# A gated recurrence and a convolutional gate on one core: fixed issue orders, tile-sized loads and word transposes

## Chip, cores and metric

One of the eight cores of a Trainium2 chip runs the kernel. The metric is the device time of one launch in microseconds. The kernel before was run 13 times: median 320.02 us, from 318.58 to 324.23. Engines are named as in the profile: PE multiplies matrices (PEld loads its weights), DVE is VectorE, ACT is ScalarE, POOL is GpSimd, and SP only issues DMAs here.

## Reference, cut to what matters

Input x and two gates are (4, 6336, 256) float32. A linear recurrence over time is followed by a gated unit whose gate is a causal convolution of five taps:

```python
log_a = 8.0 * sigmoid(r_gate) * log(clip(sigmoid(a_param), 1e-6, 1 - 1e-6))
a_t = exp(log_a)
x_gated = sqrt(maximum(1 - a_t * a_t, 1e-6)) * sigmoid(i_gate) * x
for t in range(S):
    h = a_t[:, t] * h + x_gated[:, t]
    y[:, t] = h
gate_pre = sum(conv_w[k] * shifted(y, 4 - k) for k in range(5))   # zeros before t = 0
out = (sigmoid(gate_pre) * (y @ w_val)) @ w_out
```

## The kernel before

The four sequences are laid end to end: 25344 rows of 256 values. They are cut into 51 tiles, 48 of 512 rows and 3 of 256, and the tiles into 28 chunks: 23 of two tiles (1024 rows) and five of one. Rows lie in partitions where data is loaded and stored; channels lie in partitions, in two halves h of 128, where the recurrence and the convolution run. So data is transposed by PE on the way in.

One tile or chunk goes through these operations, each a function `op_...` in the code:

- **load** (chunk, SP, L249 and L250): r_gate and i_gate into `ri`, two buffers of a chunk (NIN). **loadx** (chunk, SP, L257): x into `xt`, three buffers (NX). The pattern of r_gate, `(w p j) d -> p w j d`, gives each partition four neighbouring rows of a tile, 4 KB in one piece; that of i_gate and x, `(k p) d -> p k d`, gives it single rows of 1 KB.
- **tanh** (tile, ACT, L351): both gates at once, into bf16 rings.
- **u2** (tile): (tanh(i) + 1) * x into `uring`, bf16. A string of letters, U2, says for each tile whether DVE does it in one instruction (L360) or POOL in two (L363, L364).
- **srT** (half a chunk, PE, L332): eight bf16 transposes of 128x128 of tanh(r) into a PSUM bank; **exp** (ACT, L376) makes a of it, and puts time in order as it reads; **e** (POOL, L384) squares a.
- **sq** (batches of one to three chunks, UNITS; ACT, L388): the square root, in place in `ering`, as bf16 (`nring`). The root and tanh/exp need different function tables, so a table load (ACT_TABLE_LOAD) stands on either side of a batch.
- **nT** (tile, PE, L397): eight bf16 transposes back to rows; **xg** (DVE, L404) multiplies them into `uring`; **xT** (half a chunk, PE, L332 again): eight transposes to channels; **scan** (DVE, L425): the recurrence, from `aring` and the PSUM bank into `yring`.
- **conv** (tile, PE, L451): the five taps as products with diagonal matrices; **tg** (ACT, L459): tanh of the gate; **val** (PE, L467): y times w_val; **gv** (DVE, L477): (tg + 1) * val.
- **out** (piece of 256 rows, PE, L489): times w_out; **osb** (evicts PSUM; a string OSB says on DVE, L500, or on ACT, L502); **store** (tile, SP, L507).

w_out is halved once at the start (DVE, L313), since sigmoid(z) = (tanh(z/2) + 1) / 2.

Four PSUM banks are shared by srT, nT, xT and out. What sets the order is a planner run when the program is built: `make_jobs` lists all jobs with a duration from a table COST and what they depend on, and `make_plan` always takes the job that can start first, ties going by a table PRIO. The jobs are written out by planned start, so each engine, and SP's queue, has one fixed order and waits in it for its semaphores. The first six load jobs of the plan are issued ahead of the setup work.

Of the kernel before, what the change touches and what calls it, by code (L numbers as in the profile page):

```python
# [18 lines left out]
UNITS = [1, 2, 2, 3, 3, 3, 3, 3, 2, 2, 1, 3]  # L19
# [4 lines left out]
NIN = 2  # L24
NX = 3
# [7 lines left out]
OSB = ("ADDDDDDDDDDDDADDDDDDDDDDDDADDDDDDDDADDDDDDDDDADDDDAADDADDDDDDADDADDDDAADDAAADADADADADADADA"  # L33
       "DAAAAAAAA")

U2 = "PDPDDDDDDPDPDPDPDDPDPPPPPPPPPPPPPPPDPPPPPPPDPPPPPPP"

COST = dict(load=(0.05, 2.8), loadx=(0.02, 1.5), tanh=(0.2, 1.7), u2P=(0.25, 3.15), u2D=(0.2, 1.55), srT=(0.05, 0.45), exp=(0.35, 0.86), e=(0.1, 1.8),
            sq=(0.3, 1.71), nT=(0.05, 0.47), xg=(0.1, 0.58), xT=(0.05, 0.45), scan=(0.21, 2.14), conv=(0.2, 1.1), tg=(0.19, 0.83),
            val=(0.02, 0.93), gv=(0.15, 1.07), out=(0.02, 0.47), osbD=(0.68, 0), osbA=(0.59, 0),  # L40
            store=(0.05, 1.3))
PRIO = dict(load=5.92, loadx=5.97, store=2.53, tanh=6, exp=2.8, sq=0.42, tg=-0.32, srT=-1.6, nT=0.31, xT=3.79,
            conv=5.3, val=4.34, out=2.99, e=5.93, u2=6, xg=4.55, scan=0.36, gv=-0.61, osb=-0.99)
# [66 lines left out]
def make_jobs(sh):  # L110
# [3 lines left out]
    jobs = {op: [] for op in PRIO}  # L114
# [8 lines left out]
    for g, (_, n) in enumerate(sh.tiles):  # L123
        f = n / WIN
        c = sh.chunk_of[g]
        job("tanh", "ACT", f, [("load", c), ("u2", g - NTI)]
            + ([("srT", 2 * sh.chunk_of[g - NTR] + 1)] if g >= NTR else []))
        job("u2", "DVE" if U2[g] == "D" else "POOL", f, [("tanh", g), ("loadx", c)] + ([("xT", 2 * sh.chunk_of[g - NU] + 1)] if g >= NU else []), "u2" + U2[g])
        job("nT", "PE", f, [("sq", unit_of[c]), ("xg", g - PB["nT"])], None, 1)
        job("xg", "DVE", f, [("nT", g), ("u2", g)])  # L130
        job("conv", "PE", f, [("scan", 2 * c + 1), ("tg", g - 1)])
        job("tg", "ACT", f, [("conv", g), ("gv", g - 2)])
        job("val", "PE", f, [("scan", 2 * c + 1), ("gv", g - 1), ("conv", g)])
        job("gv", "DVE", f, [("tg", g), ("val", g)] + ([("out", qlast[g - 2])] if g >= 2 else []))
        job("store", "DMA", f, [("osb", q) for q, (w, _) in enumerate(sh.pieces) if w == g])
    for c, (_, n, g0, g1) in enumerate(sh.chunks):
        f = n / CHUNK
        job("load", "DMA", 2 * f, [("tanh", sh.chunks[c - NIN][3] - 1 if c >= NIN else -1)])
        job("loadx", "DMA", 2 * f, [("u2", sh.chunks[c - NX][3] - 1 if c >= NX else -1)])
# [20 lines left out]
def make_plan(sh):  # L160

    jobs = make_jobs(sh)
    reads = dict(exp="srT", xg="nT", scan="xT", osb="out")
    nxt = dict.fromkeys(jobs, 0)
    done, free, order, mode = {}, dict(DMA=START, ACT=ACT_START), [], "E"
    bank_free, banks = [0.0] * BANKS, {}
    while True:
        best = None  # L170
        for op, todo in jobs.items():
            i = nxt[op]
            if i == len(todo):
                continue
            eng, dur, deps, need = todo[i]
            t = free.get(eng, 0.0)
            if need:
                b = min(bank_free)
                if b == math.inf:
                    continue  # L180
                if b:
                    t = max(t, b + SEM)
            for d in deps:
                e = done.get(d)
                if e is None:
                    break
                if e + SEM > t:
                    t = e + SEM
            else:
                if best is None or (t, PRIO[op]) < best[:2]:  # L190
                    best = (t, PRIO[op], op, i, eng, dur, need)
        if best is None:
            break
        t, _, op, i, eng, dur, need = best
        if eng == "ACT" and op != "osb":
            if (op == "sq") != (mode == "S"):
                dur += TABLE
            mode = "S" if op == "sq" else "E"
        free[eng] = t + dur
        done[op, i] = t + dur + (DMA_LAT if eng == "DMA" else 0.0)  # L200
        if need:
            banks[op, i] = bank_free.index(min(bank_free))
            bank_free[banks[op, i]] = math.inf
        if op in reads:
            bank_free[banks[reads[op], i]] = t + dur
        order.append((t, op, i, eng, dur))
        nxt[op] += 1
    assert all(nxt[op] == len(todo) for op, todo in jobs.items()), nxt
    order.sort(key=lambda o: o[0])
    return order, banks  # L210
# [3 lines left out]
def kernel(  # L214
# [29 lines left out]
    def load(c):  # L244
        t0, nt, g0, g1 = chunks[c]
        nw, nj = g1 - g0, nt // (g1 - g0) // P
        ri = inp.tile([P, 2, 2, SUB, D], FP32, name="ri", tag="ri", bufs=NIN)

        nc.sync.dma_start(ri[:, 0, 0:nw, 0:nj, :], rf[t0:t0 + nt, :].rearrange("(w p j) d -> p w j d", w=nw, j=nj))  # L249
        nc.sync.dma_start(ri[:, 1, 0:nw, 0:nj, :].rearrange("p w j d -> p (w j) d"),  # L250
                          if_[t0:t0 + nt, :].rearrange("(k p) d -> p k d", p=P))
        live["ri", c] = ri

    def loadx(c):
        t0, nt, g0, g1 = chunks[c]
        xt = inp.tile([P, 2 * SUB, D], FP32, name="xt", tag="xt", bufs=NX)
        nc.sync.dma_start(xt[:, 0:nt // P, :], xf[t0:t0 + nt, :].rearrange("(k p) d -> p k d", p=P))  # L257
        live["xt", c] = xt

    with tc.manual_schedule():  # L260
# [5 lines left out]
        before = [(op, g) for _, op, g, eng, _ in plan if eng == "DMA"][:6]  # L266
# [46 lines left out]
        nc.vector.tensor_scalar(out=wo[:], in0=wo[:], scalar1=0.5, scalar2=None, op0=ALU.mult)  # L313
# [4 lines left out]
        def bank(b, dtype):  # L318
            return psum.tile([P, WIN * 4 // mybir.dt.size(dtype)], dtype, name=f"bank{b}", tag=f"bank{b}", bufs=1)
# [5 lines left out]
        uring = rings.tile([P, NU, SUB, D], BF16, name="uring")  # L325
        yring = rings.tile([P, H, NY * WIN], BF16, name="yring")

        def transposes(dst, srcs, h):
            col = 0
            for src, nj in srcs:  # L330
                for j in range(nj):
                    nc.tensor.transpose(out=dst[:, col:col + P], in_=src[:, j, h * P:(h + 1) * P],  # L332
                                        identity=ident_b[:])
                    col += P
# [9 lines left out]
        def op_tanh(g, eng):  # L344
            nj = tiles[g][1] // P
            c = chunk_of[g]
            ri, w = live["ri", c], g - chunks[c][2]
            if g == chunks[c][3] - 1:
                del live["ri", c]
            r, i = g % NTR, NTR + g % NTI  # L350
            nc.scalar.activation(out=tring[:, r:i + 1:i - r, 0:nj, :], in_=ri[:, :, w, 0:nj, :], func=ACT.Tanh, scale=0.5)  # L351

        def op_u2(g, eng):
            nj = tiles[g][1] // P
            c = chunk_of[g]
            w = g - chunks[c][2]
            xt, ti = live["xt", c][:, w * nj:(w + 1) * nj, :], tring[:, NTR + g % NTI, 0:nj, :]
            u = uring[:, g % NU, 0:nj, :]
            if eng == "DVE":
                nc.vector.scalar_tensor_tensor(out=u, in0=ti, scalar=1.0, in1=xt, op0=ALU.add, op1=ALU.mult)  # L360
                return
            t1 = work.tile([P, SUB, D], FP32, name="t1", tag="t1", bufs=1)[:, 0:nj, :]
            nc.gpsimd.tensor_scalar(out=t1, in0=ti, scalar1=1.0, scalar2=1.0, op0=ALU.mult, op1=ALU.add)  # L363
            nc.gpsimd.tensor_tensor(out=u, in0=t1, in1=xt, op=ALU.mult)  # L364

        def op_srT(k, eng):
            c, h = k // 2, k % 2
            srT = bank(banks["srT", k], BF16)
            transposes(srT, [(tring[:, g % NTR], tiles[g][1] // P) for g in range(*chunks[c][2:])], h)
# [21 lines left out]
        def op_nT(g, eng):  # L391
            c = chunk_of[g]
            n0, nt = shape.npos[c] + tiles[g][0] - chunks[c][0], tiles[g][1]
            nT = bank(banks["nT", g], BF16)[:].rearrange("p (j d) -> p j d", d=D)
            for h in range(H):
                for j in range(nt // P):
                    nc.tensor.transpose(out=nT[:, j, h * P:(h + 1) * P],  # L397
                                        in_=nring[:, h, n0 + j * P:n0 + (j + 1) * P], identity=ident_b[:])
            live["nT", g] = nT

        def op_xg(g, eng):
            nj = tiles[g][1] // P
            u = uring[:, g % NU, 0:nj, :]
            nc.vector.tensor_tensor(out=u, in0=live.pop(("nT", g))[:, 0:nj, :], in1=u, op=ALU.mult)  # L404

        def op_xT(k, eng):
            c, h = k // 2, k % 2
            xT = bank(banks["xT", k], BF16)
            transposes(xT, [(uring[:, g % NU], tiles[g][1] // P) for g in range(*chunks[c][2:])], h)
# [8 lines left out]
        def op_scan(k, eng):  # L418
# [4 lines left out]
            xT = live.pop(("xT", k))  # L423
# [59 lines left out]
        def op_out(q, eng):  # L483
            g, i = pieces[q]
            gv = live["gv", g]
            ops = bank(banks["out", q], FP32)
# [6 lines left out]
        def op_osb(q, eng):  # L493
# [5 lines left out]
            if eng == "DVE":  # L499
                nc.vector.tensor_copy(out=dst, in_=ops[:])  # L500
            else:
                nc.scalar.copy(out=dst, in_=ops[:])  # L502
# [42 lines left out]
```

## Time and profile before

One execution was profiled; it took 320.02 us, which happens to be the median, and its span from the first to the last instruction is 318.2 us.

| what | value |
|---|---|
| profiled execution | 320.02 us |
| its span | 318.2 us |
| busy ACT, DVE, PE, POOL | 290.7, 270.4, 245.8, 225.0 us |
| DMA: bytes, mean rate | 104.55 MB, 329 GB/s |
| tanh L351, 128x2048 | 48 of 1914 ns |
| e L384, 128x1024 | 46 of 1974 ns |
| u2 on POOL, L363 and L364, 128x1024 | 33 of 1161 + 2419 ns |
| u2 on DVE, L360, 128x1024 | 15 of 1646 ns |
| eviction on DVE L500, on ACT L502 | 69 of 677 ns, 30 of 584 ns |
| table loads | 26 of 1283 ns |
| scan L425, 128x1024 | 40 of 2337 ns |

How to read it: a line of the profile names line, engine, operation, output and inputs, then the count, the busy time and the mean duration. The slices cut the span in 40 equal parts of 8 us; a digit is the busy share in tenths. Lines of waits give who waited for whom, the total in us, how often, and the longest. The chain follows the work that ended last back from the end. DMA packets are the pieces that one DMA engine moves in one go; their records tell their size and how long each took.

### The profile page before, as it was taken

How to read it: one execution, taken by the hardware profiler on the slowest of the kernel's cores; microseconds unless marked ns; L12 is line 12 of the kernel's file. 1: busy time of each engine (PE TensorE's matmuls, PEld its weight loads, DVE VectorE, ACT ScalarE, POOL GpSimd, SP SyncE). 2: the span in 40 equal slices, each digit the busy share in tenths (PEclk: the TensorE clock that was granted, in tenths of full speed). 3: DMA queues.
4: the chain of work that ended last, by engine and by line, in shares of the span. 5: the costliest groups of instructions: out<-in, count | busy, mean ns of one | idle time of the engine just before them, and what ended most of it. 6: DMA issues, size and time to landing. Idle time of an engine off the chain costs nothing.

```text
span 318.2 us, 7194 instructions
## 1 busy us (share of the span) xinstructions
PE 245.8 (77%) x2954; PEld 163.3 (51%) x2987; DVE 270.4 (85%) x269; ACT 290.7 (91%) x231; POOL 225.0 (71%) x140
## 2 busy tenths in 40 slices
PE   1262976686588768897989788968977997989994
PEld 1141744453465446464746475637654665655662
DVE  3125798997789976999999989997999999999892
ACT  6789999989969899999999999899989999998963
POOL 6339550978487717999879999999997389868000
PEclk9999999999969797999999999997999999999999
DMA  8999999999999998999999999995999994753334
GB/s 206 345 363 381 366 368 382 384 384 345 392 350 343 393 367 292 320 386 388 350 386 379 397 375 383 395 390 193 381 383 393 380 387 160 255 200 134 135 150 181
DMA packets 67327, 104.55 MB, mean 329 GB/s; under 512 B 3287, under 2 KB 54238, under 8 KB 67294
## 3 DMA queue, kind: packets, MB, share of 16 engines
q1 hardware_dynamic: 65904, 103.82, 91.2%
q0 software_dynamic: 1376, 0.26, 1.0%
q8 instruction: 23, 0.38, 0.5%
q14 instruction: 10, 0.08, 0.1%
q10 hardware_dynamic: 14, 0.01, 0.0%
HBM read 78.39 MB, written 25.95 MB: 328 GB/s over the span
## 4 chain that ended last, share of the span: by engine, by line
ACT 26%; DMA 22%; DVE 19%; issue 13%; PE 12%; POOL 4%; SPq 1%; DVEq 0%; ACTq 0%; POOLq 0%
DMA ri<-in_i_gate_dram 14%; DVE yring L425 9%; ACT tring L351 7%; DMA xt<-in_x_dram 6%; ACT ering L388 6%; DVE gv L477 5%; PE gp L451 4%; ACT tg L459 4%; PE bank L489 4%; ACT aring L376 3%; DVE osb L500 2%; POOL uring L364 2%; DMA ri<-in_r_gate_dram 2%; DVE uring L404 2%; ACT L388 2%
## 5 line engine op out<-in xcount | busy, mean ns | idle before, releaser
L384 POOL TENSOR_TENSOR ering<-aring 128x1024 f32<-128x1024 f32 (+2 forms) x56 | 97.5, 1761 | 56.2 <-ACT aring L376 54.4
L425 DVE TENSOR_TENSOR_SCAN yring<-aring,yring,bank 128x1024 bf16<-128x1024 f32 (+5 forms) x54 | 110.0, 2050 | 0.7 <-PE bank L332 0.5
L351 ACT ACTIVATE tring<-ri 128x2048 bf16<-128x2048 f32 (+1 forms) x51 | 93.8, 1864 | 6.2 <-DMA ri<-in_i_gate_dram 6.1
L364 POOL TENSOR_TENSOR uring<-t,xt 128x1024 bf16<-128x1024 f32 (+1 forms) x36 | 83.6, 2323 | 9.6 <-DMA xt<-in_x_dram 6.9
L451 PE MATMUL gp<-yring,diag 64*64 64x512 bf16 (+14 forms) x1196 | 69.6, 356 | 5.5 <-ACT tg L459 3.9
L489 PE MATMUL bank<-wo,gv 128*128 128x256 bf16 x396 | 57.4, 279 | 17.8 <-DVE gv L477 7.5
L477 DVE SCALAR_TENSOR_TENSOR gv<-tg,val 128x1024 bf16<-128x1024 bf16 (+1 forms) x54 | 60.1, 1118 | 8.2 <-ACT tg L459 6.0
L376 ACT ACTIVATE aring<-bank,khf 128x1024 f32<-128x1024 bf16 (+2 forms) x56 | 59.5, 1108 | 3.7 <-PE bank L332 3.0
L459 ACT ACTIVATE tg<-gp 128x1024 bf16<-128x1024 f32 (+1 forms) x51 | 51.0, 1001 | 8.6 <-PE gp L451 8.3
L489 PEld LDWEIGHTS <-gv 128*128 128x128 bf16 x396 | 36.1, 99 | 37.2 <-issue 16.3
L467 PE MATMUL val<-yring,wv 128*128 128x512 bf16 (+1 forms) x171 | 46.3, 375 | 2.9 <-DVE gv L477 1.0
L451 PEld LDWEIGHTS <-diag 64*64 64x64 bf16 x1196 | 31.4, 111 | 32.9 <-issue 16.4
L500 DVE COPY osb<-bank 128x512 f32<-128x512 f32 x69 | 45.4, 677 | 2.4 <-PE bank L489 1.9
L388 ACT ACTIVATE ering<-ering,b 128x2048 bf16<-128x2048 f32 (+4 forms) x15 | 46.7, 3112 | 0.5 <-POOL ering L384 0.3
L332 PE MATMUL bank<-ident_b,tring 128*128 128x128 bf16 x396 | 31.6, 233 | 17.5 <-ACT tring L351 12.7
L397 PE MATMUL bank<-ident_b,ering 128*128 128x128 bf16 x396 | 31.7, 234 | 17.0 <-ACT ering L388 14.8
L404 DVE TENSOR_TENSOR uring<-bank,uring 128x1024 bf16<-128x1024 bf16 (+1 forms) x51 | 33.3, 667 | 13.1 <-PE bank L397 12.7
L363 POOL TENSOR_SCALAR t<-tring 128x1024 f32<-128x1024 bf16 (+1 forms) x36 | 40.2, 1116 | 2.6 <-ACT tring L351 1.2
L332 PEld LDWEIGHTS <-tring 128*128 128x128 bf16 x396 | 26.1, 104 | 26.7 <-ACT tring L351 14.4
L397 PEld LDWEIGHTS <-ering 128*128 128x128 bf16 x396 | 26.8, 106 | 24.7 <-ACT ering L388 15.8
L332 PE MATMUL bank<-ident_b,uring 128*128 128x128 bf16 x396 | 30.9, 227 | 4.4 <-DVE yring L425 1.8
L360 DVE SCALAR_TENSOR_TENSOR uring<-tring,xt 128x1024 bf16<-128x1024 bf16 x15 | 24.7, 1646 | 8.1 <-DMA xt<-in_x_dram 8.1
(32 smaller groups left out, 112.6 us busy)
## 6 DMA issues: line engine op xcount, KB each, us to landing
out_dram<-osb SPq DMA_DIRECT2D x48, 512.0 KB, 6.8
ri<-in_r_gate_dram SPq DMA_DIRECT2D x23, 1024.0 KB, 8.1
ri<-in_i_gate_dram SPq DMA_DIRECT2D x23, 1024.0 KB, 10.9
xt<-in_x_dram SPq DMA_DIRECT2D x23, 1024.0 KB, 10.6
ri<-in_r_gate_dram SPq DMA_DIRECT2D x2, 512.0 KB, 6.0
ri<-in_i_gate_dram SPq DMA_DIRECT2D x2, 512.0 KB, 7.9
xt<-in_x_dram SPq DMA_DIRECT2D x2, 512.0 KB, 8.2
ri<-in_r_gate_dram SPq DMA_DIRECT2D x3, 256.0 KB, 3.1
```

Source lines behind the costliest of these rows:

```text
L332: nc.tensor.transpose(out=dst[:, col:col + P], in_=src[:, j, h * P:(h + 1) * P], identity=ident_b[:])
L351: nc.scalar.activation(out=tring[:, r:i + 1:i - r, 0:nj, :], in_=ri[:, :, w, 0:nj, :], func=ACT.Tanh, scale=0.5)
L364: nc.gpsimd.tensor_tensor(out=u, in0=t1, in1=xt, op=ALU.mult)
L376: nc.scalar.activation(out=aring[:, h, a0:a0 + nt].rearrange("c (w p j) -> c w p j", p=P, j=nj), in_=live.pop(("srT", k))[:, 0:nt].rearran ...
L384: nc.gpsimd.tensor_tensor(out=ering[:, h, e0:e0 + nt], in0=a, in1=a, op=ALU.mult)
L388: nc.scalar.activation(out=nring[:, :, 2 * e0:2 * e0 + m], in_=ering[:, :, e0:e0 + m], func=ACT.Sqrt, scale=-0.25, bias=b025[:, 0:1])
L397: nc.tensor.transpose(out=nT[:, j, h * P:(h + 1) * P], in_=nring[:, h, n0 + j * P:n0 + (j + 1) * P], identity=ident_b[:])
L425: nc.vector.tensor_tensor_scan(out=yring[:, h, y0 + c0:y0 + c1], data0=aring[:, h, a0 + c0:a0 + c1], data1=xT[:, c0:c1], initial=0.0 if fr ...
L451: nc.tensor.matmul(out=gp[64 * h:64 * h + 64, m, c0:c1], lhsT=diag[rows, h, kk, rows], rhs=yring[rows, h, src:src + c1 - c0], start=(sh == 0),
L459: nc.scalar.activation(out=tg[:, :, 0:nt], in_=live.pop(("gp", g))[:, :, 0:nt], func=ACT.Tanh, scale=0.5)
L477: nc.vector.scalar_tensor_tensor(out=gv[:, 0:nj, hs, :].rearrange("c j h p -> c j (h p)"), in0=tg[:, hs, 0:nt].rearrange("c h (p j) -> c j ...
L489: nc.tensor.matmul(out=ops[:, e * D:(e + 1) * D], lhsT=gv[:, 2 * i + e, hk, :], rhs=wo[:, hk, :], start=(hk == 0), stop=(hk == H - 1))
```

## The change

It has these parts:

1. **Orders.** The planner that chose by start time and priority is gone. In its place each engine has a string of letters (ORDER), and each use of a shared PSUM bank a digit (BANK_ORDER). `make_plan` only replays them to merge the five orders into one. OSB gives ACT 25 pieces in place of 30, U2 gives DVE 8 tiles in place of 15, UNITS swaps its first two batches.
2. **Loads by tile.** load and loadx move one tile each, all three inputs with four neighbouring rows to a partition (4 KB in one piece). There are four buffers of a tile for the gates and five for x. The first eight load jobs are issued ahead of the setup.
3. **Word transposes.** Since the rows of x now lie as those of r_gate, two neighbouring bf16 values in `uring` (the same channel in two neighbouring rows) and in `nring` (two neighbouring steps) form a 4-byte word. nT and xT transpose these words as float32, four instructions of 128x128 in place of eight. In nT the weights are read with a step of two words; in xT the words are written to PSUM with a step of two. srT stays in bf16.
4. **u2 writes in pairs.** On DVE it is two instructions, whose inner two elements are read 256 elements apart; on POOL the product stores bf16 with a step of two elements.
5. **The half.** w_out is no longer halved at the start; the eviction multiplies by 0.5 (`tensor_scalar` on DVE, an activation Copy with a scale on ACT).

The diff, cut to its core:

```diff
-UNITS = [1, 2, 2, 3, 3, 3, 3, 3, 2, 2, 1, 3]
+UNITS = [2, 1, 2, 3, 3, 3, 3, 3, 2, 2, 1, 3]
-NIN = 2
-NX = 3
+NIN = 4
+NX = 5
...
-U2 = "PDPDDDDDPDPDPDPDDPDPPPPPPPPPPPPPPPPDPPPPPPPDPPPPPPP"
+U2 = "DDPDDDPPDPPPPDPPPPPPPPPPPPPPDPPPPPPPPPPPPPPPPPPPPPP"
...
+LETTERS = dict(
+    DMA=dict(l="load", x="loadx", s="store"), ACT=dict(t="tanh", e="exp", q="sq", g="tg", o="osb"),
+    PE=dict(r="srT", n="nT", x="xT", c="conv", v="val", o="out"), POOL=dict(e="e", u="u2"),
+    DVE=dict(u="u2", x="xg", s="scan", v="gv", o="osb"))
+ORDER = dict(
+    DMA=("llllxllxxxllxlxlxxxlxllxxsllxlsxxsslxlxslllsxxllssxxslslxlxxslslxsslxlxlxsxllsxlxsxsxlxsllxslxlslssx"
+         "xlsxslxllssxsxxsllxlslsxxsxxsslsxlxslsssxxsssssssssss"),
+    ACT=("teetetteeetqqttgeteetegtqegtetgetetgeettgqgetteogoetgtegtgeegtgqettegetgteegetgqgttgeetgtgetegeettgq"
+         "getgettgeetgeetgtgqetgetgeettgeogqgtgetgetegtqogeoeogootgqgtteegoeogeeoeogqogoogoooggogooogogoo"),
...
-        job("tanh", "ACT", f, [("load", c), ("u2", g - NTI)]
+        job("load", "DMA", f, [("tanh", g - NIN)])
+        job("loadx", "DMA", f, [("u2", g - NX)])
+        job("tanh", "ACT", f, [("load", g), ("u2", g - NTI)]
...
+    def load(g):
+        t0, nt = tiles[g]
+        nj = nt // P
+        ri = inp.tile([P, 2, SUB, D], FP32, name="ri", tag="ri", bufs=NIN)
+        for k, src in enumerate((rf, if_)):
+            nc.sync.dma_start(ri[:, k, 0:nj, :], src[t0:t0 + nt, :].rearrange("(p j) d -> p j d", j=nj))
+        live["ri", g] = ri
...
-        before = [(op, g) for _, op, g, eng, _ in plan if eng == "DMA"][:6]
+        before = [(op, g) for _, op, g, eng, _ in plan if eng == "DMA"][:8]
...
-        nc.vector.tensor_scalar(out=wo[:], in0=wo[:], scalar1=0.5, scalar2=None, op0=ALU.mult)
...
+            u = uring[:, g % NU, 0:nj * D].rearrange("p (w d e) -> p w d e", d=D, e=2)
             if eng == "DVE":
-                nc.vector.scalar_tensor_tensor(out=u, in0=ti, scalar=1.0, in1=xt, op0=ALU.add, op1=ALU.mult)
+                xk = xt.rearrange("p (w e) d -> p w d e", e=2)
+                tk = ti.rearrange("p (w e) d -> p w d e", e=2)
+                for k in range(nj // 2):
+                    nc.vector.scalar_tensor_tensor(out=u[:, k], in0=tk[:, k], scalar=1.0, in1=xk[:, k], op0=ALU.add,
+                                                   op1=ALU.mult)
...
-            nc.gpsimd.tensor_tensor(out=u, in0=t1, in1=xt, op=ALU.mult)
+            nc.gpsimd.tensor_tensor(out=u.rearrange("p w d e -> p w e d"), in0=t1.rearrange("p (w e) d -> p w e d", e=2),
+                                    in1=xt.rearrange("p (w e) d -> p w e d", e=2), op=ALU.mult)
...
+            nT = bank(banks["nT", g])
             for h in range(H):
-                for j in range(nt // P):
-                    nc.tensor.transpose(out=nT[:, j, h * P:(h + 1) * P],
-                                        in_=nring[:, h, n0 + j * P:n0 + (j + 1) * P], identity=ident_b[:])
+                for w in range(nw):
+                    nc.tensor.transpose(out=nT[:, w * D + h * P:w * D + (h + 1) * P],
+                                        in_=ering[:, h, n0 + w:n0 + nw * P:nw], identity=ident_f[:])
...
+            for g in range(*chunks[c][2:]):
+                nw = tiles[g][1] // P // 2
+                for w in range(nw):
+                    nc.tensor.transpose(out=xT[:, at + w:at + nw * P:nw],
+                                        in_=uring_w[:, g % NU, w * D + h * P:w * D + (h + 1) * P], identity=ident_f[:])
+                at += nw * P
...
-                nc.vector.tensor_copy(out=dst, in_=ops[:])
+                nc.vector.tensor_scalar(out=dst, in0=ops[:], scalar1=0.5, scalar2=None, op0=ALU.mult)
             else:
-                nc.scalar.copy(out=dst, in_=ops[:])
+                nc.scalar.activation(out=dst, in_=ops[:], func=ACT.Copy, scale=0.5)
```

## Prediction

> **What bounds the kernel now.** I read the busy line first, then the slices, the queues, the chain, the waits of ScalarE, and last the stretches. Busy line, slices and queue:
>
> ```profile
> PE 245.8 (77%) x2954; PEld 163.3 (51%) x2987; DVE 270.4 (85%) x269; ACT 290.7 (91%) x231; POOL 225.0 (71%) x140
> ...
> ACT  6789999989969899999999999899989999998963
> POOL 6339550978487717999879999999997389868000
> ...
> DMA  8999999999999998999999999995999994753334
> ...
> DMA packets 67327, 104.55 MB, mean 329 GB/s; under 512 B 3287, under 2 KB 54238, under 8 KB 67294
> ...
> q1 hardware_dynamic: 65904, 103.82, 91.2%
> ```
>
> ScalarE (ACT) is the busiest engine, 290.7 of 318.2 us, and the DMA engines are at 9 from slice 2 to 33: two limits side by side until about 265 us. After that the loads are over and DMA falls to 3 or 4. The reader is to see that 54238 of 67327 packets are under 2 KB: nearly all are the 1 KB packets of i_gate and x.
>
> The chain and ACT's waits:
>
> ```profile
> ACT 26%; DMA 22%; DVE 19%; issue 13%; PE 12%; POOL 4%; SPq 1%; DVEq 0%; ACTq 0%; POOLq 0%
> ```
> ```profile
> ACT tg L459 <- PE gp L451: 8.3, 11, 1.5
> ACT tring L351 <- DMA ri<-in_i_gate_dram: 6.1, 6, 1.9
> ACT aring L376 <- PE bank L332: 3.0, 6, 1.2
> ```
>
> The chain changes engine all the time, so no one engine's stall is the answer; DMA has 22% of it because gate loads queue behind other transfers for some 10 us. Yet ACT itself loses only 6.1 us to DMA. Busy time by stretch (PE, PEld, DVE, ACT, POOL; then clock, DMA share, GB/s):
>
> ```profile
> 0.00:18.00 18.00, 5.00 (x43) 3.34 (x43) 5.11 (x21) 12.41 (x14) 10.03 (x18) 1.00 1.00 290
> 18.00:100.00 82.00, 56.71 (x618) 38.70 (x621) 64.81 (x58) 77.93 (x55) 52.71 (x26) 0.96 1.05 367
> 100.00:200.00 100.00, 83.29 (x1045) 55.01 (x1055) 92.98 (x90) 95.85 (x68) 82.42 (x48) 0.97 1.03 369
> 200.00:265.00 65.00, 55.54 (x705) 37.39 (x712) 62.16 (x57) 61.52 (x48) 55.34 (x32) 0.97 0.98 358
> 265.00:300.00 35.00, 32.34 (x385) 20.46 (x390) 33.64 (x30) 33.52 (x36) 24.47 (x19) 1.00 0.47 168
> 300.00:318.20 18.20, 12.92 (x169) 8.40 (x168) 11.73 (x17) 9.47 (x15) 0.00 (x0) 1.00 0.43 171
> ```
>
> ACT's 27.5 us without work are 5.6 before 18 us, 13.2 between 18 and 300, and 8.7 after. Added up by releaser from the trace's records, the middle 13.2 is 8.5 behind PE, 3.4 behind DMA, 1.3 small. So I account for the time on ACT: busy plus three idles.
>
> **Loads.** r_gate and the stores already move 4 KB packets. In the trace's packet records a 1 KB packet takes 49.6 ns in the mean (median 46), a 4 KB packet 165.9 (159). The 50688 packets of 1 KB become 12672 of 4 KB: 2512.6 us of packet time become 12672 x 165.9 ns = 2102, over 16 engines 25.7 us less. The queue's 91.2% of 318.2 = 290 us falls to 264, about 86% of a span of 307: DMA stops being a limit. Of this, only ACT's 3.4 us of middle DMA waits lie on my path; the rest frees cover. The 2.6 us of DMA waits at the start stay, since the first gate loads are bound by size. SP issues 204 transfers in place of 135; plain ones cost it 0.36 us each, 73 us in all, hidden under 300. One wait is added: x has five tiles of room where it had three chunks (six tiles), so a load of x waits for u2 five tiles back, and gate loads queued behind it on SP hold up tanh. Cover is the four gate tiles ahead, 4 x 5.8 us of ACT's work.
>
> The transfers halve to 512 KB. Stores of that size are in the trace, and after 260 us, where stores prevail, 4 KB packets still take 159 ns in the median; I cost the halving at nothing. The Trainium skill, "DMA: Bandwidth & Descriptors", Rules for kernel authors, speaks against it: it wants at least 1 MiB per DMA. By its 341 GB/s at 1 MB all 104.55 MB would need an estimated 307 us and the kernel would stay near 320; the slices here show up to 397 GB/s with transfers queued back to back, so I go by the row.
>
> **ACT's work.** OSB gives ACT 25 evictions for 30: 5 x 584 ns = 2.9 us less. In the new order twelve square roots stand in eleven places (two adjacent), so one pair of table loads goes: 2 x 1283 ns = 2.6. Copy with a scale in place of copy I cost at the same 584; no table load follows an L502 copy here, and if each new Copy drew one, it would be 25 x 1.28 = 32 us or more. So 285.2 us of work.
>
> **DVE and POOL.** Seven u2 move from DVE to POOL. DVE: -7 x 1646 ns, +5 evictions x 677, -0.3 for wo: 8.4 us less, and the eight u2 left there are cut in two with a strided read (between nothing and double: 0 to 13 us; I take 0.2 each, near the row 1646). DVE stays near 264, not the bound. POOL: +7 x (1161 + 2419) ns = 25, so 250. All 43 u2 there now store bf16 with a step of 4 bytes, which no row shows. Bounds: 0 (L384, the same engine's plain product, takes 1974) to half as much again, 1.2 us each. I take 0, nearest to the contiguous row. Cover: POOL's last work ends 24 us before the end, and a steady tile costs it 1.05 + 2.36 + 1.90 = 5.3 us by medians against ACT's 285.2 / 49.5 = 5.8.
>
> **PE.** 792 bf16 transposes of 128 columns become 396 of fp32 words. The bf16 ones end 56 ns apart when packed. The only fp32 ones, the two of L305 (5 columns), end 106 ns apart. Bounds: 396 x 56 = 22 us (22 less than 792 x 56 = 44), and four passes, 396 x 224 = 89 (44 more). I take 106: 42 us, equal; a group of four then takes the 0.45 us that eight take. The words of xT are written to PSUM two words apart. The trace has no strided PSUM write, and I cost it inside 106 ns. The skill, "Advanced Engine Details and Errata", PSUM Cachelines, speaks against this part: any non-contiguous pattern "significantly slows down matmuls". It gives no figure; if it doubled the time of xT's 198, PE would have an estimated 21 us more, half of rival 4 below.
>
> **Order and tail.** Each engine still runs in a fixed order. After the last square root ACT had five tg and ten evictions, and idled; the new order puts seven tg and sixteen evictions there, some 17 us of work (with the table load) in place of 11. The tail's chain of scan, conv, tg, gv, out, store sets its length, so this moves work into idle time. Bounds: 0 to 5.3 us (8.7 less the 3.4 of the last store). I take half, 2.7. ACT's 8.5 us behind PE I leave: a new order can shift them either way.
>
> **Sum.** 318.2 - 2.9 - 2.6 - 3.4 - 2.7 = 306.6 of span. The profiled execution took 320.02 (1.8 beyond its span), which is also the median: 308.4.
>
> **Rivals.**
> 1. *ACT paced, as above.* For: 95% busy from 18 to 265 us, and DVE, POOL and DMA all get less full or stay below. With no middle idle but 4 us and 3.4 at the end: 285.2 + 5.6 + 4 + 3.4 + 1.8 = 300. With 6 us more lost to stalls: 314.
> 2. *The order gives it back.* Fixed orders wait where durations differ from the model; ACT's 8.5 us behind PE become 15 to 20, or x loads block SP: 314 to 322. For: the longest single wait in the chain is a queued load. Against: nothing in the profile favours the old order.
> 3. *POOL becomes the bound (slower).* The stepped bf16 store in u2. POOL needs 250 + 43d, about 15 us at the start and 24 after its last work; that passes 306.6 from d = 0.41 us on and the old span from d = 0.68 (28%). At half as much again, 250 + 51 + 39 + 1.8 = 342; at 0.8 us 325. Against: the reads stay contiguous.
> 4. *Four passes per word transpose.* PE at 245.8 + 44 = 290 us, with nT and xT groups 0.45 us later each: some 12 to 20 us back on ACT, 320 to 328.
> 5. *The Copy draws table loads:* 308.4 + 32 = 340.
>
> **Numbers.** Chances: rival 1 0.62, rival 2 0.16, rival 3 0.11, rival 4 0.07, rival 5 0.04. A difference of 0.5% (1.6 us) is about what a measurement of this kernel can tell from none. Faster: all of 1, half of 2 and a little of 4, 0.71. Same: 0.09. Slower: 0.20. The range runs from 300, the floor of rival 1, to 324, which takes in rival 2 and the near halves of 3 and 4.
>
> **What would show it.** Right: DMA packets near 29000, DMA digits of 8 and less from the middle on, queue q1 near 264 us; ACT busy near 285 with 24 table loads; ACT's waits for ri gone after 18 us; POOL near 250, its u2 product near 2.4 us; word transposes 106 ns apart. Wrong: POOL at 9 throughout with a u2 product above 2.8 us; word transposes 200 ns apart and ACT waiting for bank; more table loads than 24; SP waiting long for u2 with tanh behind it. If DMA remains at 9 with 4 KB packets slower than 166 ns, the first step is wrong.

## The result, and the profile after

The changed kernel takes **326.49 us** (median of 11 runs, 324.28 to 329.99) against 320.26 us of the kernel before, run beside it (48 runs): a ratio of 1.0206, with a 95% interval of 1.0177 to 1.0235. It is slower by 2%, where 308.4 us were predicted and 324 was the top of the range. Ratios, here and below, leave out executions over 1.5% above the fastest of their kernel, medians do not. The profiled execution took 326.49 us, its span is 324.7.

The page of the changed kernel, the same lines as before (busy time, slices, packets, queue):

```profile
PE 249.6 (77%) x2561; PEld 162.2 (50%) x2591; DVE 269.1 (83%) x273; ACT 285.8 (88%) x224; POOL 245.0 (75%) x154
...
ACT  5699699599999999999999989999957999779644
...
DMA  7999995997999699999977999999799749443345
...
DMA packets 30797, 104.51 MB, mean 322 GB/s; under 512 B 4391, under 2 KB 4654, under 8 KB 30766
...
q1 hardware_dynamic: 29376, 103.82, 84.2%
...
ACT 36%; PE 20%; DVE 19%; issue 11%; DMA 8%; POOL 4%; SPq 2%; ACTq 0%; DVEq 0%; POOLq 0%
```

What the change takes away is gone: ACT works 4.9 us less, the packets are fewer than half, DMA has fallen from 22% of the chain to 8%. Yet the span is 6.5 us longer, so ACT idles 38.9 us in place of 27.5. In the chain PE went from 12% to 20%. ACT's waits in the changed kernel (us in total, times, longest):

```profile
ACT tg L476 <- PE gp L468: 16.4, 13, 3.3
...
ACT aring L387 <- PE bank L378: 9.6, 9, 2.4
...
ACT tring L353 <- DMA ri<-in_i_gate_dram: 1.9, 2, 1.4
```

The first was 8.3, the second 3.0, the third 6.1. Waits for data became waits for PE. But PE has hardly more to do than before (249.6 us against 245.8), so the reader must ask what PE waits for:

```profile
PE bank L408 <- ACT ering L399: 18.7, 7, 6.0
...
DVE gv L494 <- PE val L484: 9.3, 7, 6.0
```

L408 is nT, L399 the square root. The first line's longest wait, 6.0 us, is a needed one: at 25 us the first nT waits for the first batch. DVE's 6.0 us for val are another matter and are found below. Most of the time went in the last three stretches (PE, PEld, DVE, ACT, POOL; clock, DMA share, GB/s):

```profile
200.00:265.00 65.00, 54.11 (x565) 35.35 (x572) 57.85 (x59) 59.07 (x41) 54.96 (x32) 0.95 0.88 328
265.00:300.00 35.00, 31.34 (x310) 19.50 (x314) 30.00 (x24) 30.00 (x34) 25.44 (x20) 0.95 0.59 205
300.00:324.70 24.70, 20.21 (x231) 12.18 (x231) 18.05 (x23) 12.62 (x20) 0.00 (x0) 0.96 0.46 185
```

ACT does 59.07 and 30.00 us in the first two, 61.52 and 33.52 before, and the tail lasts 24.7 us in place of 18.2. Added up from the start, ACT's work is 3.1 us behind that of the kernel before at 100 us, 2.1 at 200, 4.5 at 265 and 8 at 300, where 4.9 us are work that it no longer has. All engines lose together, as they do when one waits in an order that the others depend on. The largest stall there, seen from PE (start, duration, instruction, idle before it):

```profile
231.13 0.60 PE L506 MATMUL bank<-wo,gv 128*128 128x256 bf16 x4
236.89 1.13 PE L408 MATMUL bank<-ident_f,ering 128*128 128x128 f32 x4 [5.16 <-ACT ering L399]
238.24 1.06 PE L484 MATMUL val<-yring,wv 128*128 128x512 bf16 x2 [0.22 <-issue]
```

and from ACT:

```profile
207.83 5.42 ACT L399 ACTIVATE ering<-ering,b 128x6144 bf16<-128x6144 f32 x1
...
232.80 4.04 ACT L399 ACTIVATE ering<-ering,b 128x2048 bf16<-128x2048 f32 x2
236.85 1.28 ACT L476 ACT_TABLE_LOAD   x1
241.47 1.02 ACT L476 ACTIVATE tg<-gp 128x1024 bf16<-128x1024 f32 x1 [3.34 <-PE gp L468]
```

The nT at 236.89 is that of tile 36. Its roots are in batch 7, which ended at 213.25. It starts when batch 8 ends, at 236.84: it waits for a square root that it does not read. Behind it in PE's order stand val of tile 32, for which DVE waits 5.99 us, and the conv of tile 33, for whose tg ACT then waits 3.34 us.

Where the pieces lie in the ring tells when PE stands there. Batch 8's second run is one instruction over both channel halves of the ring, bf16 elements 0 to 1023 and 8192 to 9215 of a partition. nT of tile 36 reads elements 2048 to 2559 of the first half, which lie **between** the two, and it reads them as float32 words, with a step. It waits for the end of that run, although no byte is shared. nT of tile 45 shows the same within one job. Batch 10, which it does not read, writes elements 6144 to 7167 and 14336 to 15359:

```profile
274.50 0.39 PE L408 MATMUL bank<-ident_f,ering 128*128 128x128 f32 x2
277.70 0.50 PE L408 MATMUL bank<-ident_f,ering 128*128 128x128 f32 x2 [2.81 <-ACT ering L399]
```

The first two transposes read elements 3584 to 4095, below both pieces, and do not wait. The other two read 11776 to 12287, between them, and wait until batch 10 ends at 277.65. A third such wait, 1.62 us for batch 1, stands before the second half of the first nT at 27.29.

The order puts five nT (tiles 0, 1, 36, 37 and 45) behind batch 1, 8 or 10 in the program, which are not their own. In the kernel before, no nT stood behind a later batch than its own.

### The profile page after: what moved, and what is told of

Same layout as the page of the kernel before. It is cut to its first block, busy times and chain, and to the rows that moved or that the text cites. A ratio compares the mean times of both kernels' runs of the same rounds, so it can differ in the third digit from the quotient of the medians.

```text
span 324.7 us, 6571 instructions
## 1 busy us (share of the span) xinstructions
PE 249.6 (77%) x2561; PEld 162.2 (50%) x2591; DVE 269.1 (83%) x273; ACT 285.8 (88%) x224; POOL 245.0 (75%) x154
## 2 busy tenths in 40 slices
DMA packets 30797, 104.51 MB, mean 322 GB/s; under 512 B 4391, under 2 KB 4654, under 8 KB 30766
## 3 DMA queue, kind: packets, MB, share of 16 engines
q1 hardware_dynamic: 29376, 103.82, 84.2%
## 4 chain that ended last, share of the span: by engine, by line
ACT 36%; PE 20%; DVE 19%; issue 11%; DMA 8%; POOL 4%; SPq 2%; ACTq 0%; DVEq 0%; POOLq 0%
ACT tring L353 11%; ACT ering L399 9%; DVE yring L442 8%; PE gp L468 6%; ACT aring L387 6%; ACT tg L476 5%; DMA xt<-in_x_dram 4%; PE bank L408 4%; DVE gv L494 4%; DMA ri<-in_i_gate_dram 3%; PE bank L506 3%; DVE osb L517 3%; PE val L484 3%; ACT L399 3%; DVE uring L364 2%
## 5 line engine op out<-in xcount | busy, mean ns | idle before, releaser
L369 POOL TENSOR_TENSOR uring<-t,xt 128x1024 bf16<-128x1024 f32 (+1 forms) x43 | 100.8, 2344 | 4.3 <-DMA xt<-in_x_dram 0.8
L468 PE MATMUL gp<-yring,diag 64*64 64x512 bf16 (+15 forms) x1196 | 68.6, 357 | 3.2 <-ACT tg L476 3.0
L387 ACT ACTIVATE aring<-bank,khf 128x1024 f32<-128x1024 bf16 (+2 forms) x56 | 60.9, 1112 | 10.3 <-PE bank L378 9.6
L494 DVE SCALAR_TENSOR_TENSOR gv<-tg,val 128x1024 bf16<-128x1024 bf16 (+1 forms) x54 | 60.5, 1124 | 10.7 <-PE val L484 9.3
L506 PE MATMUL bank<-wo,gv 128*128 128x256 bf16 x396 | 58.5, 277 | 11.4 <-DVE osb L517 4.1
L408 PE MATMUL bank<-ident_f,ering 128*128 128x128 f32 x198 | 35.7, 310 | 24.9 <-ACT ering L399 18.7
L517 DVE TENSOR_SCALAR osb<-bank 128x512 f32<-128x512 f32 x74 | 48.8, 680 | 5.0 <-DMA out_dram<-osb 2.4
L484 PE MATMUL val<-yring,wv 128*128 128x512 bf16 (+1 forms) x174 | 48.5, 382 | 3.6 <-DVE gv L494 1.5
L399 ACT ACTIVATE ering<-ering,b 128x2048 bf16<-128x2048 f32 (+3 forms) x15 | 46.7, 3113 | 0.3
L368 POOL TENSOR_SCALAR t<-tring 128x1024 f32<-128x1024 bf16 (+1 forms) x43 | 45.1, 1049 | 2.0
L408 PEld LDWEIGHTS bank<-ident_f,ering 128*128 128x128 f32 x198 | 28.1, 207 | 32.4 <-ACT ering L399 21.7
L424 PE MATMUL bank<-ident_f,uring 128*128 128x128 f32 x198 | 33.2, 289 | 6.5 <-DVE uring L415 4.5
L364 DVE SCALAR_TENSOR_TENSOR uring<-tring,xt 128x512 bf16<-128x512 bf16 x15 | 19.7, 1358 | 16.6 <-DMA xt<-in_x_dram 16.6
```

The costliest lines, as they stand in the source:

```text
L369: nc.gpsimd.tensor_tensor(out=u.rearrange("p w d e -> p w e d"), in0=t1.rearrange("p (w e) d -> p w e d", e=2), in1=xt.rearrange("p (w e) ...
L387: nc.scalar.activation(out=aring[:, h, a0:a0 + nt].rearrange("c (w p j) -> c w p j", p=P, j=nj), in_=live.pop(("srT", k))[:, 0:nt].rearran ...
L399: nc.scalar.activation(out=nring[:, :, 2 * e0:2 * e0 + m], in_=ering[:, :, e0:e0 + m], func=ACT.Sqrt, scale=-0.25, bias=b025[:, 0:1])
L408: nc.tensor.transpose(out=nT[:, w * D + h * P:w * D + (h + 1) * P], in_=ering[:, h, n0 + w:n0 + nw * P:nw], identity=ident_f[:])
L468: nc.tensor.matmul(out=gp[64 * h:64 * h + 64, m, c0:c1], lhsT=diag[rows, h, kk, rows], rhs=yring[rows, h, src:src + c1 - c0], start=(sh == 0),
L494: nc.vector.scalar_tensor_tensor(out=gv[:, 0:nj, hs, :].rearrange("c j h p -> c j (h p)"), in0=tg[:, hs, 0:nt].rearrange("c h (p j) -> c j ...
```

## The experiments

Theory A: the time lost is such needless waits, made by word transposes that read the ring as float32 and by an order that did not know of them. Rival B: the new data path itself (word transposes, paired u2, 4 KB loads) costs time. Rival C: the x loads and their place in SP's order.

| kernel | what differs | median us | ratio to before, interval |
|---|---|---|---|
| after | | 326.49 | 1.0206 [1.0177, 1.0235] |
| a_x_early | x loaded earlier | 327.7 | 1.0186 [1.0115, 1.0256] |
| a_sq_split | batches 1, 8, 10 in halves | 315.78 | 0.9814 [0.9766, 0.9863] |
| a_both | both of these | 315.23 | 0.9809 [0.9776, 0.9843] |
| a_s1 | batch 1 alone | 324.66 | 1.0102 [0.999, 1.0214] |
| a_s8 | batch 8 alone | 320.04 | 0.9969 [0.9924, 1.0014] |
| a_s10 | batch 10 alone | 321.45 | 1.0044 [0.9997, 1.0091] |
| a_split_1k | splits, 1 KB packets | 316.69 | 0.9858 [0.98, 0.9916] |
| a_nopair | DVE's u2 plain | 320.25 | 0.9998 [0.9972, 1.0024] |
| a_split_nopair | splits, DVE's u2 plain | 308.39 | 0.962 [0.9586, 0.9654] |
| a_oldpath | old data path, no split | 310.73 | 0.9686 [0.9649, 0.9723] |
| a_split_oldpath | old data path, splits | 310.0 | 0.9645 [0.9596, 0.9694] |
| a_mixed | splits, old path for DVE's tiles | 310.59 | 0.9676 [0.9644, 0.9708] |
| b_words | before, new data path | 326.21 | 1.0113 [1.005, 1.0176] |
| b_words2 | the same again | 328.02 | 1.0149 [1.0091, 1.0207] |
| b_nopair | b_words, DVE's u2 plain | 317.46 | 0.9857 [0.9793, 0.992] |

a_split_1k, b_nopair, a_nopair and a_split_nopair move and work on as much data as the others, but their values are not the reference's: rows or channels are paired that do not belong together.

**Data path or order? b_words and a_x_early.** b_words is the kernel before with the loads, word transposes and paired u2 of the change; its chunks, planner and strings stay.

```diff
-        nc.sync.dma_start(... "(k p) d -> p k d")           # i_gate and x
+        nc.sync.dma_start(... "(w p j) d -> p w j d")
...  op_u2, op_nT, op_xg, op_xT, op_scan as in the kernel after
```

> The kernel before with the data path of the change alone: 4 KB packets for all three inputs, paired u2, word transposes for nT and xT; loads by chunk, planner, engine choices and the halving of w_out as before. Theory A (the order is at fault, the data path is sound): faster than before by what the DMA waits and queued loads cost, 312 to 318 us, ACT's waits for ri near nothing, DMA digits below 9. Theory B (the word transposes and the paired u2 are at fault, since their instructions are longer): 321 to 328 us, with ACT's waits for gp and bank near the 16 and 10 us of the kernel after.

Measured 326.21 us: the new data path makes the old order slower. That spoke for B. Its profiled execution took 588.61 us and is not read here; b_words2 below is the same kernel again.

```diff
-    DMA=("llllxllxxxllx...
+    DMA=("llxlxllxlxllx...
```

> The kernel after with one change in SP's order: its first thirteen loads are l l x l x l l x l x l l x in place of l l l l x l l x x x l l x, so the first two loads of x come 1 and 3 places earlier or more. Theory A: DVE's wait of 10.0 and 6.6 us for the first x falls to some 6 and 2, and the end comes 2 to 5 us sooner, 321 to 324.5 us. Theory B: the start is not on the path, 325.5 to 327.5.

Measured 327.7 us: nothing is won. What x gains the gate loads lose: ACT idles 8.1 us before 18 us, in place of 5.9. C is out.

**The needless waits: a_sq_split and a_both.** The square root of a batch goes in two instructions, one for each channel half, so that nothing lies between.

```diff
+SPLIT = (1, 8, 10)
-                nc.scalar.activation(out=nring[:, :, 2 * e0:2 * e0 + m], in_=ering[:, :, e0:e0 + m], ...
+                for hs in ([slice(0, 1), slice(1, 2)] if u in SPLIT else [slice(0, H)]):
+                    nc.scalar.activation(out=nring[:, hs, 2 * e0:2 * e0 + m], in_=ering[:, hs, e0:e0 + m], ...
```

> The kernel after with the square roots of three batches (1, 8 and 10) issued one channel half at a time, so that the wait of a transpose nT for a later batch, whose two halves span its words without touching them, is gone. Costs ACT four instructions, about 1 us. Theory A: PE no longer sits 5.2 us ahead of nT at 232 us, the end comes 3 to 6 us sooner, 320.5 to 323.5 us. Theory B: 326 to 328.

> The kernel after with both: x loads earlier and the three square root batches split. Theory A: the gains add, 316 to 320 us, at or under the kernel before. Theory B: 325.5 to 327.5.

Measured 315.78 and 315.23 us: with three splits 10.7 us less than after, more than was expected, and less than both kernels. The earlier x loads add nothing to it. (Kernels run in different groups stand beside a kernel before of 320.26 to 321.88 us; by the ratios, 1.0206 - 0.9814, it is 3.9% or 12.5 us.) In a_sq_split PE's and ACT's timelines at the same place read:

```profile
228.04 0.60 PE L508 MATMUL bank<-wo,gv 128*128 128x256 bf16 x4
228.56 0.75 PE L410 MATMUL bank<-ident_f,ering 128*128 128x128 f32 x4
229.14 1.03 PE L486 MATMUL val<-yring,wv 128*128 128x512 bf16 x4
```
```profile
229.72 4.28 ACT L401 ACTIVATE ering<-ering,b 128x1024 bf16<-128x1024 f32 x4
234.01 1.28 ACT L478 ACT_TABLE_LOAD   x1
235.31 1.02 ACT L478 ACTIVATE tg<-gp 128x1024 bf16<-128x1024 f32 x1
```

nT (L410) now starts before batch 8 does, val follows at once, and tg comes right behind the table load, with no idle time. All three waits are gone, 9.6 us together, and of nT's waits for roots the needed ones are left:

```profile
PE bank L410 <- ACT ering L401: 9.3, 4, 6.0
```

Four halves take 4.28 us where two whole runs took 4.04: a split costs 0.24 us here.

**One batch at a time: a_s8, a_s1, a_s10.** SPLIT is (8,), (1,) and (10,).

> The kernel after with only batch 8 of the square root issued one channel half at a time. Theory A (each needless wait costs what PE stands at it, and the costs add): PE's wait of some 5 us before nT36 at 232 us goes, and the time falls by 5 to 6 us, to 320.5 to 321.5. Rival B (one place makes nearly all of the 10.7 us that the three splits gave together): 316 to 318 here, and next to nothing in the other two. Rival C (nothing adds: a stall that goes in one place comes back in the next): 324 or more.

> The kernel after with only batch 1 of the square root issued one channel half at a time. Theory A: the 1.6 to 2.1 us that PE stands before nT0's second half at 27 us go, and with it some of the start's lag: 2 to 3.5 us less, 323 to 324.5. Rival B and C: 325.5 to 327, since a start that is earlier only waits for loads later, as the earlier x loads showed.

> The kernel after with only batch 10 of the square root issued one channel half at a time. Theory A: the 3 to 4 us that the engines fall behind the plan between 280 and 296 us go: 322.5 to 324. Rival B and C: 325.5 to 327.

Measured 320.04, 324.66 and 321.45 us: 6.5, 1.8 and 5.0 us less. Medians of so few runs carry 1 to 2 us of scatter; within one execution the stretch between two instructions of ACT tells it better (us, from the trace's records):

| from, to (ACT) | after | a_s1 | a_s8 | a_s10 | a_sq_split |
|---|---|---|---|---|---|
| exp of half chunk 2, tanh of tile 16 | 75.4 | 73.3 | 75.8 | 75.3 | 73.7 |
| tg of tile 32, exp of half chunk 46 | 21.1 | 21.1 | 15.4 | 21.1 | 15.4 |
| tg of tile 39, osb of piece 80 | 20.1 | 20.1 | 21.3 | 16.2 | 16.2 |

Each split shortens its own stretch and no other: 1.7 to 2.1 us for batch 1, 5.7 for batch 8, 3.9 to 5.1 for batch 10. They add up to 11.3 to 12.9, against 10.7 (12.5 by the ratios) measured together. Theory A stands; that one place makes it all does not. Of a stall that comes back in the next there is little: with batch 8 alone split, the third stretch is 1.2 us longer.

**Are 4 KB packets worth anything? a_split_1k.**

```diff
+            rows = "(p j) d -> p j d" if k == 0 else "(j p) d -> p j d"      # x: "(j p) d -> p j d"
```

> The three splits, but i_gate and x are loaded as before, single rows to a partition in packets of 1 KB; the rows of i_gate and x then stand in another order than those of r_gate, so what is multiplied isn't the reference's; all else is the same. It prices the 4 KB packets alone under the new order. Theory A (the loads' 25.7 us of queue time were cover and 3.4 us of waits): 318 to 322, 3 to 6 us above the 315.8 of the three splits. Rival D (the loads set the time once the order is tight): queue time 297 to 300 us of the span with transfers late throughout, 324 or more. Rival E (packet size makes no difference): 315 to 317.

Measured 316.69 us, against 315.78 with 4 KB, with intervals that overlap: rival E. The queue is busy 93.5% of 312.5 us = 292 us, 21 more than the 86.9% of 312.0 = 271 of a_sq_split, and ACT waits for ri 2.9 us in all, most of it at the start. Under this order, at 316 us, the loads are cover whichever packets carry them; at the 308 us reached below that was not tried alone.

**Words or halves? b_words2, b_nopair, a_split_oldpath.** b_nopair gives DVE one plain u2 instruction:

```diff
-                for k in range(nj // 2):
-                    nc.vector.scalar_tensor_tensor(out=u[:, k], in0=tk[:, k], scalar=1.0, in1=xk[:, k], ...
+                nc.vector.scalar_tensor_tensor(out=uring[:, g % NU, 0:nj * D].rearrange("p (j d) -> p j d", d=D), in0=ti, ...
```

a_split_oldpath keeps the new orders, loads by tile, the half in the eviction and the splits, and takes op_u2, op_nT, op_xg and op_xT from the kernel before, with the loads of a_split_1k.

> The same kernel as b_words once more (the kernel before with 4 KB loads, word transposes and paired u2, everything else old), for a profile that can be read: its first profiled execution was disturbed. Time again 324 to 327. Theory F (DVE pays: its 15 u2 in two halves take 2.4 to 2.7 us in place of 1.65, DVE busy 281 to 286, its scans and products later, ACT's waits for PE up by some 5 us). Theory G (PE pays: its word transposes hold a bank longer, DVE near 272, ACT's waits for bank up).

> b_words2, but DVE's 15 u2 are one plain instruction each as in the kernel before; the words that xT transposes there then hold two neighbouring channels, so for these 15 tiles what reaches the recurrence isn't the reference's. POOL's 36 tiles are paired as before. Theory F: DVE gets its 12 us back and the time falls to 319 to 322, that of the kernel before or a little less. Theory G: no change, 324 to 327.

> The new orders, the loads by tile, the half in the eviction and the three splits, with the old data path: i_gate and x in 1 KB packets, u2 plain on both engines, nT and xT as eight transposes in bf16. With 1 KB packets alone the splits gave 316.7 us; what differs here is words and pairs. Theory H (words and pairs are worth nothing where ACT sets the time): 315 to 318. Theory F (DVE's eight u2 in halves cost time here too): 311 to 314.5. Theory I (words spare PE time that ACT waits for): 319 or more. If H, the whole change of the data path is worth about nothing, and orders, splits and spared work of ACT make all of the gain.

Measured 328.02, 317.46 and 310.0 us. In the old order the halves alone cost some 9 us (by the ratios, 1.0149 - 0.9857; the medians are 10.6 apart), more than expected: DVE is busy 284.2 us with them (in an execution of 328.79 us) and 272.6 without. With plain u2 the rest of the data path makes the old order 1.4% faster. Under the new order the whole old data path is 6.7 us faster than a_split_1k, more than theory F asked for. The word transposes are not to blame in b_nopair, which has them.

Why halves cost so much is seen in DVE's and POOL's timelines of the kernel after:

```profile
47.44 3.87 DVE L364 SCALAR_TENSOR_TENSOR uring<-tring,xt 128x512 bf16<-128x512 bf16 x2
51.23 0.68 DVE L517 TENSOR_SCALAR osb<-bank 128x512 f32<-128x512 f32 x1
51.83 3.72 DVE L364 SCALAR_TENSOR_TENSOR uring<-tring,xt 128x512 bf16<-128x512 bf16 x2
```
```profile
46.93 2.35 POOL L369 TENSOR_TENSOR uring<-t,xt 128x1024 bf16<-128x1024 f32 x1
49.37 1.39 POOL L368 TENSOR_SCALAR t<-tring 128x1024 f32<-128x1024 bf16 x1
50.84 2.69 POOL L369 TENSOR_TENSOR uring<-t,xt 128x1024 bf16<-128x1024 f32 x1
53.62 1.38 POOL L368 TENSOR_SCALAR t<-tring 128x1024 f32<-128x1024 bf16 x1
```

Two halves take 3.87 us; apart from POOL a half takes 0.69, and a whole u2 of the kernel before 1.20 to 1.21. The first starts at 47.44 while POOL's product runs to 49.28, and by the records ends at 49.85. The second starts beside POOL's next instruction, which runs to 50.76, and ends at 51.30. All seven halves that begin under a POOL instruction and take over 1.4 us end 0.54 to 0.56 us after it; of the kernel before, whole u2 that begin so end about 1.08 us after it. So a u2 on DVE, whose two inputs both lie in SBUF, waits for the POOL instruction in progress and then does its work; the eviction at 51.23, which reads PSUM, takes its usual 0.68 beside POOL. POOL pays too: its L368 takes 1.39 us beside a half, against 1.05 free. Two instructions can meet two.

The Trainium skill says so, "SBUF — State Buffer", section SBUF: two separate sides: DVE and GpSimd share a pair of ports, and of a DVE op with two SBUF inputs and a GpSimd op that reads SBUF "whichever" starts first has it "for the whole instruction". The trace agrees, with 0.55 us between the ends.

**Do the two causes make up the whole? a_split_nopair, a_oldpath, a_nopair.** The edits are those above: plain u2 on DVE with and without the splits, and a_split_oldpath with an empty SPLIT.

> The kernel after with the three splits, and DVE's eight u2 as one plain instruction each; the words that xT transposes then hold two neighbouring channels in these eight tiles, so what reaches the recurrence there isn't the reference's. 4 KB loads, word transposes and POOL's paired u2 stay. Theory F (DVE's halves cost the 6 us: a half that starts beside a POOL instruction ends 0.55 us after it, and two halves wait for two): DVE 263 us busy, 309 to 312. Theory G (word transposes hold the banks longer): 314 to 316.5, as with the splits alone.

> New orders, loads by tile and the half in the eviction with the old data path, and no split: the needless waits for the square root are back. Theory A (the waits cost the same with either data path): 310.0 + 10.7 = 320 to 322, so the orders alone are worth nothing as they stand. Rival C (they cost less where DVE isn't late): 313 to 317.

> The kernel after with nothing changed but DVE's eight u2, one plain instruction each (in these tiles not the reference's values, as in a_split_nopair); no split. If the two costs add: 326.5 less some 6 us, 319.5 to 322. If DVE's halves only cost time where the square root's waits are gone: 325 to 327.

Measured 308.39, 310.73 and 320.25 us. Plain u2 is worth 6.2 us without the splits and 7.4 with them; splits and plain u2 together 18.1, the sum of the two alone 16.9 (by the ratios 18.8 and 19.2). They add: theory A holds, and of rival B the u2 cut in two.

a_oldpath missed what theory A expected of it, and makes the theory sharper. Without any split it takes 310.73 us: with the old data path the splits are worth nothing that shows (310.0 with them, and the intervals overlap). The three stretches above take 70.9, 15.2 and 16.0 us in it. Its PE and ACT where batch 8 stands:

```profile
226.62 0.61 PE L406 MATMUL bank<-ident_b,ering 128*128 128x128 bf16 x8
227.06 1.03 PE L482 MATMUL val<-yring,wv 128*128 128x512 bf16 x4
```
```profile
227.77 4.04 ACT L396 ACTIVATE ering<-ering,b 128x2048 bf16<-128x2048 f32 x2
```

nT's waits for roots in it are the needed ones again, as in a_sq_split:

```profile
PE bank L406 <- ACT ering L396: 9.5, 5, 6.0
```

The order is that of the kernel after, each run of the square root is one instruction over both halves, and nT does not wait: it reads the ring as bf16, the type in which the root was written, and without a step. The needless wait comes only with the word transposes, which read it as float32 and with a step; no run tells these two apart. That the program takes all that lies between the two pieces for written is a reading of this; where the waits are and what takes them away is shown. So the wait belongs to the data path **and** to the order: b_words has the words without an nT behind a later batch, a_oldpath such an nT without the words.

**A version that computes the reference: a_mixed.** The three splits; the eight tiles with u2 on DVE take the old data path, the other 43 the new one.

```diff
+            rows = "(j p) d -> p j d" if k and U2[g] == "D" else "(p j) d -> p j d"
...
+            if U2[g] == "D":            # u2 plain; nT and xT in bf16
```

> The kernel after with the three splits, and the eight tiles whose u2 runs on DVE on the old data path (i_gate and x in 1 KB rows, u2 in one plain instruction, nT and xT in bf16); the other 43 tiles keep 4 KB loads, word transposes and POOL's paired u2. It computes the reference. If the needless waits and DVE's halves are the whole excess: 307 to 310, no slower than the old data path throughout (310.0). If word transposes or 4 KB loads cost something of their own where DVE is free: 311 or more.

Measured 310.59 us, between the two expectations and no better than the old data path. Of the versions that compute the reference, a_mixed, a_split_oldpath and a_oldpath are best, and not told apart; all beat both kernels by some 3% or more. Why a_mixed does not reach a_split_nopair's 308.4 stays open; its eight tiles differ in loads and transposes at once.

## Why the prediction was wrong

ACT's account (busy, idle before 18 us, idle up to 18.2 us from the end, idle in the last 18.2 us), from the records:

| | busy | start | middle | last 18.2 us | span |
|---|---|---|---|---|---|
| predicted | 285.2 | 5.6 | 9.8 | 6.0 | 306.6 |
| after | 285.8 | 5.9 | 22.6 | 10.3 | 324.7 |
| a_split_nopair | 285.2 | 5.7 | 5.6 | 10.5 | 307.1 |
| a_oldpath | 284.8 | 7.7 | 6.6 | 10.6 | 309.7 |

- **The step that failed** is "ACT's 8.5 us behind PE I leave: a new order can shift them either way". They became 20.8 (11.4 behind gp, 9.4 behind a bank). This is what rival 2 named, "ACT's 8.5 us behind PE become 15 to 20", but its causes, durations that differ from the model and x loads that block SP, are not what made this loss: an earlier place for x wins nothing. The cause is the wait of nT for a foreign batch, 11 to 12 us of the kernel's time. The orders' own model has no such wait. Rival 2's top of 322 allowed for one such loss and not for the next.
- **The eight u2 cut in two**, "between nothing and double: 0 to 13 us; I take 0.2 each", were the second failure. Seven are cut; tile 0, of 256 rows, is one instruction. A cut tile costs DVE 2 x 1358 ns = 2.7 us, where the model in the kernel has 1.9: here durations did differ. All eight take 19.7 us, against 13.2 plain (a_split_nopair): 6.5 us more where 1.6 were taken, and DVE was busy 269.1 us, not 264. Nor is it hidden: 6.2 us of the kernel's time. "DVE stays near 264, not the bound" priced a busy share. By the waits a late DVE holds PSUM banks: ACT's for a bank fall from 9.4 to 5.1 us when u2 is plain (a_nopair).
- **Loads.** Packets, queue and 4 KB time were right in kind (30797 packets; 84.2% of 324.7 = 273 us, 264 predicted), and the middle's DMA waits went. But not because of the packets: a_oldpath has 1 KB packets and 0.4 us of such waits in the middle (a_split_oldpath 1.8), and b_nopair, with 4 KB packets in the old order, has 4.4, where the kernel before had 3.4. Orders and loads by tile, which no run separates, remove them.
- **ACT's work** was right: 285.8 us, 24 table loads, none for the Copy. Rival 5 is out. "No table load follows an L502 copy here" was read wrong: six of the 30 copies have one right behind them, but each belongs to a change to or from a square root.
- **POOL**: u2's product takes 2396 ns, 2419 before; a stepped bf16 store costs nothing, and POOL is busy 245.0 us. Rival 3 is out.
- **PE**: word transposes end 120 ns (nT) and 108 to 110 ns (xT) apart, 106 predicted; two words of step in PSUM cost nothing that shows, since xT, which has it, is the faster of the two. Rival 4 is out.
- **Tail**: 2.7 us of gain were taken, none came; the last 18.2 us hold 10.3 us of idle time, 8.8 before. After the last square root the new order has thirteen evictions, not the sixteen of the prediction. a_split_nopair still meets the predicted 308.4 us, but by luck: its middle is 4.2 us better than predicted and its tail 4.5 worse, and it is not the kernel that was predicted.

With both causes away (a_split_nopair) the time is 308.39 us, and with the data path left as it was (a_oldpath) 310.73. So of the change the orders, the loads by tile and ACT's spared work are worth about 10 us; the new data path is worth some 2 under these orders, and as it was wired in it costs 16.

## What to carry to other kernels

When a static order is searched on a model, look in the built program for waits that the model doesn't have, above all where one instruction writes two far-apart pieces and another reads between them through a view of another type. Compare each instruction's start with its planned time: the lag rises in steps, and each step is one place to look at. In the kernel after, ACT's tanh, exp, tg and evictions are some 10 us behind `make_plan`'s times from 67 to 150 us, 13 at 226, 19 at 253 and 23 at 290; in a_oldpath they are never more than 10 us behind. And count the meetings of DVE and POOL before an instruction is cut in two, since each piece can wait for a POOL instruction of its own.

## What the runs showed of the hardware that was not expected

- A DVE u2 half takes 0.69 us alone and up to 2.86 beside POOL; under a POOL instruction it ends 0.55 us after it.
- 512 KB loads in 4 KB packets reach up to 419 GB/s in slices of a_sq_split, 1 KB packets up to 400 in a_split_1k, and the times, 315.78 and 316.69 us, are not told apart.
- A square root over 2048 columns in two halves costs 0.12 us more than in one instruction, so a split is cheap where it frees another engine.
